# A product with wv by seven block products instead of eight, on one core

## The chip, the core and the metric

The kernel runs on one core of a Trainium2 chip. The core has TensorE (PE, matrix products), VectorE (DVE), ScalarE (ACT), GpSimd (POOL), SyncE (SP, which here only issues transfers) and 16 DMA engines. Each engine works through its own queue in order; semaphores make one wait for another. Products land in PSUM, which has eight banks of 128 x 512 numbers of 32 bits; everything else lies in SBUF. The metric is the device time in microseconds (us) of one execution.

## What is computed

Attention in blocks, a token and channel mixer, and a gated block follow each other. For 4 batches of 576 tokens with 512 channels:

```python
x = attention(q, k, v)                           # 8 heads of 64, mask by blocks of 64
xt = x.transpose(0, 2, 1)
h = np.maximum(xt @ w_tok1, 0.0) @ w_tok2
u = x + h.transpose(0, 2, 1)
u = u + np.maximum(u @ w_ch1, 0.0) @ w_ch2
x_prev = np.concatenate([zeros, u[:, :-1, :]], axis=1)
xk = mu_k * u + (1.0 - mu_k) * x_prev
xr = mu_r * u + (1.0 - mu_r) * x_prev
k = np.maximum(xk @ w_k, 0.0)                    # 512 to 1024
v = k * k @ w_v                                  # 1024 to 512
r = 1.0 / (1.0 + np.exp(-(xr @ w_r)))
return (r * v).astype(np.float32)
```

The change is in the line of v.

## The kernel before

**Tiling.** Channels lie on partitions, tokens along the row. The 2,304 tokens are eight tiles `t` of T = 288, two per batch; `u[b]` holds a batch's activations. Every dense product is done three times with numbers split into a high and a low part (high x high, high x low, low x high), by `dense`: three matmuls of 128 x 128 weights on 128 x 288 operands for each block of 128 channels.

**Weights.** They arrive from the host as 64-bit numbers, in pages of 128 rows and 512 columns. `page_ops` makes each page into a high and a low part: a load on SP (`l`), two conversions (`d0` on ACT or POOL, `d1` on ACT), the packing on DVE in two instructions (`d2`, lines 453 and 454), an addition on POOL (`d3`, line 458), the rounded copy (`hi`, line 182 on POOL, 178 on ACT) and the subtraction (`lo`, line 185, on DVE or POOL). Pages c1 and c2 are the channel mixer's, k, r and v the last block's. The last block's pages take the places of the channel mixer's as those come free.

**The last block.** For each tile: `xa` and `xm` (lines 757 and 761) mix neighbouring tokens, the result is split (`xsh`, `xsl`); K is eight blocks of 12 matmuls, `KR` the relu (line 786), `KS` the square (790), `KH` and `KL` its high and low part (797); R is four blocks of 12, `SG` the sigmoid; V is four blocks of 24 matmuls (`VO` for the first tile, by page: eight blocks of 12), and `Y` (843) multiplies V from PSUM with the sigmoid and sends it out. In TensorE's order a tile is K, R, V.

**Order.** Nothing is issued in the order of the code. `Plan` keeps a list of operations with engine, cost, dependences and priority, and lays them out one after another: of those that can start first on an engine, the one with the smallest priority number, to which the table `TILT` adds an offset by kind. Operations that may run on two engines go where the plan sees them end. Rings (PSUM banks, buffers) are resources of the plan. `record` then writes each engine's instructions in that order.

**PSUM.** The attention stage and the first channel-mixer tile use six single banks and one double bank (`ps1`); then `change2` releases them and a pool of eight banks follows.

Of the kernel before, what the change touches and what calls it, by code (L numbers as in the profile page):

```python
# [22 lines left out]
T = 288  # L23
# [22 lines left out]
TILT = {"ku": -1.2, "h1h": 0.5, "xl": -1.4, "n": -4.5, "h1l": -5.2, "xh": -1.6, "page-t2": 2.9, "xt": -0.6, "v": -2.0, "k2": 1.2, "q": 0.5, "rc": -3.6, "KH": 3.7, "KL": 0.2, "R": -1.5, "xa": 1.9, "page-v": 3.0, "O": 0.2, "V": -0.1, "Lh": -4.5, "xsh": -3.8, "U": -0.1, "C2": -4.8, "t": -14.0, "xm": 7.3, "K": 3.9, "z": 0.9, "page-c2": 4.3, "page-k": -1.7, "Ll": 13.8, "KS": -1.6, "page-c1": 2.6, "page-t1": -1.5, "xsl": 0.8, "load": 0.2, "L": 3.3, "e": 2.3, "page-r": -1.9, "pv": -0.2, "KR": -0.6, "m": -0.2}  # L46
# [6 lines left out]
class Plan:  # L53
# [8 lines left out]
    def __init__(self, tc):  # L62
        self.tc, self.last = tc, {}
        self.ops, self.users, self.rings, self.mode, self.slot = {}, {}, {}, {}, {}
# [4 lines left out]
    def add(self, name, engine, cost, deps, fn, pri, alloc=(), uses=(), lat=None, mode="f"):  # L69
# [3 lines left out]
        if kind in ("l", "d0", "d1", "d2", "d3", "hi", "lo"):  # L73
            kind = "page-" + name[1]
        elif kind == "v" and len(name) == 2:
            kind = "load"
# [35 lines left out]
    def run(self):  # L112
# [8 lines left out]
        self.taken = {t: [None] * n for t, n in self.rings.items()}  # L121
        self.order = []
# [47 lines left out]
def attn_mixer_rwkv_kernel(ctx: ExitStack, tc: tile.TileContext, z, v, wt1, wt2, wc1, wc2, wk, wv, wr, mu, out):  # L170
# [42 lines left out]
    u = [glob.tile([128, 4, S + 1], F32, name=f"u{b}") for b in range(B)]  # L213
# [23 lines left out]
    tl = {}  # L237


    def warm(k):  # L240
        t = ps1.tile([128, 512], F32, tag="s", bufs=6, name="warm")
# [23 lines left out]
    plan.ring("one", 6)  # L265
# [91 lines left out]
    def emit_pv(p, chunks):  # L357
        vt, vx = vs[p % 3], vd[p % 3]
        for i in chunks:
            part = int(i == 0)  # L360
            if ("pv", p, part) not in tl:
                tl["pv", p, part] = ps1.tile([128, 512], F32, tag="s", bufs=6, name="pv")
# [97 lines left out]
    def page_ops(name, src, n, room, pri, split_pri=None, gate=(), alloc=(), dense=False, late=False, slack=0.0):  # L460
# [28 lines left out]
        add(("hi",) + name, ("ACT", "POOL") if dense else "POOL", {"ACT": c_act(c), "POOL": c_pool1(c)}, [("d3",) + name], hi, sp, alloc=alloc, uses=[tk], lat=0.15 + 0.1 * slack)  # L489
# [408 lines left out]
```

## Time and profile before

| | |
|---|---|
| three runs, median (lowest to highest) | 820.31 us (819.71 to 820.81) |
| the profiled execution, its time | 821.57 us |
| its span, first to last instruction | 819.8 us |
| TensorE matmuls busy | 797.8 us (97%), 6,608 instructions |
| VectorE busy | 454.1 us (55%) |
| ScalarE busy | 355.5 us (43%) |
| GpSimd busy | 268.8 us (33%) |
| mean granted TensorE clock | 0.989 |

The stages in the trace: attention and the token mixer up to about 228 us, the channel mixer up to 548 us, the last block from there. Busy time counts the time in which an instruction runs; an instruction that has started and waits for access counts as busy too. An average over the span says little: the stages have different limits, so the windows by stretch and the waits of a stretch are read. A matmul's record of 0.3 us is its latency; the distance from one start to the next is the price.

### The profile page before, as it was taken

What the parts mean: (1) busy time and instruction counts of PE and PEld (TensorE: products, weight loads), DVE (VectorE), ACT (ScalarE), POOL (GpSimd) and SP (SyncE); (2) the same over time, 40 slices, a digit from 0 to 9 for tenths busy, and PEclk for the clock granted to TensorE, in tenths of its full rate; (3) what the DMA queues carried; (4) which work ended last, traced back from release to release, by engine and by line L of the source; (5) the groups of instructions that cost most, each with busy time, mean ns of one, the idle gap of its engine ahead of it and who ended that gap; (6) DMA issues with size and microseconds to landing.
All of it is one profiled execution on the core that took longest, in us unless ns stands there. A gap on an engine that the chain in (4) does not pass through costs nothing. (4 is left out here: it accounts for less than half of the span.)

```text
span 819.8 us, 16500 instructions
## 1 busy us (share of the span) xinstructions
PE 797.8 (97%) x6608; PEld 774.7 (95%) x6608; DVE 454.1 (55%) x1119; ACT 355.5 (43%) x913; POOL 268.8 (33%) x347
## 2 busy tenths in 40 slices
PE   7999999999998999999999999999699999999998
PEld 6898999999998989999999999998699999999998
DVE  5888877767777782212112124888963463553640
ACT  4786767666634451211111121444562362452530
POOL 4777764564666781101010102666400000000000
PEclk9999999999999999999999999999799999999999
DMA  6444323332124431000000000332000000000000
GB/s 175 136 128 138 99 79 106 98 89 90 37 71 152 156 123 58 1 1 2 1 1 1 1 2 27 104 105 102 26 6 30 22 10 30 15 15 30 9 22 30
DMA packets 34109, 47.60 MB, mean 58 GB/s; under 512 B 12912, under 2 KB 25200, under 8 KB 34032
## 3 DMA queue, kind: packets, MB, share of 16 engines
q1 hardware_dynamic: 34032, 46.54, 18.0%
q8 instruction: 52, 0.85, 0.4%
q14 instruction: 25, 0.20, 0.1%
HBM read 41.82 MB, written 4.72 MB: 57 GB/s over the span
## 5 line engine op out<-in xcount | busy, mean ns | idle before, releaser
L188 PE MATMUL b<-xhl,w 128*128 128x288 f32 x2304 | 312.4, 296 | 0.4 <-POOL xhl L686 0.4
L188 PEld LDWEIGHTS b<-xhl,w 128*128 128x128 f32 x2304 | 309.5, 188 | 0.6 <-POOL xhl L686 0.6
L188 PE MATMUL b<-hh,w 128*128 128x288 f32 x768 | 157.4, 298 | 4.5 <-DVE w L185 3.0
L188 PEld LDWEIGHTS b<-hh,w 128*128 128x128 f32 x768 | 125.1, 190 | 5.4 <-DVE w L185 3.7
L711 ACT ACTIVATE hh<-b 128x288 fp32r<-128x288 f32 x96 | 39.4, 410 | 191.6 <-PE b L188 191.1
L188 PE MATMUL b<-kh,w 128*128 128x288 f32 x512 | 106.0, 300 | 8.4 <-POOL w L182 3.7
L188 PE MATMUL b<-hl,w 128*128 128x288 f32 x384 | 113.8, 296 | 0.0
L339 POOL TENSOR_SCALAR P<-P,st 128x320 f32<-128x320 f32 (+4 forms) x160 | 85.6, 554 | 67.7 <-ACT P L330 38.6
L330 ACT ACTIVATE P<-P,st 128x576 f32<-128x576 f32 (+4 forms) x160 | 88.5, 556 | 20.3 <-DVE st L325 18.8
L188 PEld LDWEIGHTS b<-kh,w 128*128 128x128 f32 x512 | 83.9, 191 | 9.8 <-POOL w L182 4.3
L714 DVE SCALAR_TENSOR_TENSOR hl<-b,hh 128x288 fp32r<-128x288 f32 x96 | 43.3, 454 | 74.2 <-ACT hh L711 73.8
L458 POOL TENSOR_TENSOR td<-td,raw 128x512 int32<-128x512 int32 (+2 forms) x53 | 66.3, 1251 | 53.3 <-DVE td L454 12.1
L188 PE MATMUL b<-kl,w 128*128 128x288 f32 x256 | 76.3, 298 | 0.0
L188 PEld LDWEIGHTS b<-hl,w 128*128 128x128 f32 x384 | 73.0, 190 | 0.0
L786 ACT ACTIVATE kr<-b 128x288 f32<-128x288 f32 x64 | 26.2, 410 | 91.3 <-PE b L188 91.0
L746 DVE TENSOR_TENSOR u<-b,u 128x288 f32<-128x288 f32 x32 | 14.1, 455 | 92.2 <-PE b L188 92.1
L686 POOL TENSOR_TENSOR xhl<-u,xhl 128x1152 fp32r<-128x1152 f32 x8 | 19.6, 2454 | 136.8 <-ACT xhl L683 136.8
L188 PE MATMUL cs<-z 64*128 64x64 f32 (+6 forms) x352 | 61.6, 357 | 0.0
L843 DVE TENSOR_TENSOR o<-b,sg 128x288 f32<-128x288 f32 x32 | 14.4, 457 | 72.0 <-PE b L188 72.0
L348 PE MATMUL pt<-ident,P 128*128 128x128 f32 x320 | 47.9, 281 | 3.0 <-POOL P L339 3.0
L325 DVE CUSTOM_DVE_ANT_0 P<-cs,mask 128x448 f32<-128x448 f32 (+3 forms) x128 | 49.5, 415 | 2.1 <-PE cs L188 1.8
L454 DVE SCALAR_TENSOR_TENSOR td<-raw,td 128x512 uint32<-128x512 uint32 (+2 forms) x53 | 48.2, 910 | 1.8
(82 smaller groups left out, 1251.9 us busy)
## 6 DMA issues: line engine op xcount, KB each, us to landing
raw<-in_wc SPq DMA_DIRECT2D x24, 512.0 KB, 3.4
z<-in_z SPq DMA_DIRECT2D x16, 576.0 KB, 3.7
out<-o SPq DMA_DIRECT2D x32, 144.0 KB, 1.8
vs<-in_v SPq DMA_DIRECT2D x16, 256.0 KB, 3.2
raw<-in_wk SPq DMA_DIRECT2D x8, 512.0 KB, 3.2
raw<-in_wv SPq DMA_DIRECT2D x8, 512.0 KB, 3.2
vd<-in_v SPq DMA_DIRECT2D x32, 80.0 KB, 3.1
raw<-in_wr SPq DMA_DIRECT2D x4, 512.0 KB, 3.3
```

What stands on the lines that cost most here:

```text
L188: PE.matmul(o, lhsT=l, rhs=r, start=start, stop=stop)
L325: DVE.tensor_tensor_reduce(p_view(p, h, i), s_view(p, h, i), m, -0.125, 3.0e38, ALU.add, ALU.min, tl["st", p, h][:, 0, i:i + 1])
L330: ACT.activation(w, w, ACTF.Exp, bias=st[:, 0, i:i + 1], scale=-1.0, accum_out=st[:, 1, i:i + 1])
L339: POOL.tensor_scalar(w, w, tl["st", p, h][:, 2, i:i + 1], 1.0, ALU.mult, ALU.mult)
L348: PE.transpose(t[:, o + 128 * k:o + 128 * k + 128], tl["P", p, i][:, c:c + 128], ident)
L454: DVE.scalar_tensor_tensor(td, hw, 0x80000000, td, ALU.bitwise_and, ALU.bitwise_or)
L458: POOL.tensor_tensor(td.bitcast(I32), td.bitcast(I32), lw, ALU.add)
L686: POOL.tensor_tensor(tl["xhl"][i][:, 1], src(), f32(tl["xhl"][i][:, 0]), ALU.subtract)
L711: ACT.activation(tl["h", t, f][0], tl["lb", t, f][:, 0:T], ACTF.Relu)
L714: DVE.scalar_tensor_tensor(tl["h", t, f][1], tl["lb", t, f][:, 0:T], 0.0, f32(tl["h", t, f][0]), ALU.max, ALU.subtract)
L786: ACT.activation(tl["kr", t, f], tl["kb", t, f][:, 0:T], ACTF.Relu)
L843: DVE.tensor_tensor(o, src, tl["sg", t, m], ALU.mult)
```

## The change

The product of a batch's squared k (1,024 x 576) with wv is cut in quadrants: k by halves of the 1,024 channels and by the two token tiles (B11, B12, B21, B22), wv by halves of its rows and columns. Seven products of quadrants, `PROD`, replace eight. Their operands are B11, B21, B22, the differences T1 = B12 - B11, T2 = B22 - T1, T3 = B22 - B12, T4 = B21 - T2 (`TS`), and sums of wv's quadrants (`weight_sums`, made once, two pages at a time; `vc` and `vd` are the new pages). Each product is 4 x 2 blocks of three matmuls. The products are added up in `u` (`EV`: `s1`, `u2`, `u3`, `c11` and so on), and `Y` multiplies there, after R. In TensorE's order a batch is now K of two tiles, seven products, R of two tiles.

`u` of the first batch gives its place to `vd`: it is sent to the output (`spill`) and fetched back into the second batch's place (`fetch`), so the batches run as 1, 2, 3, 0. `bank` takes all PSUM tiles from one ring of eight; the change of pools is gone. wv's pages are decoded ahead of wr's. `TILT` has new numbers for nearly all kinds, among them these:

```diff
-TILT = {"ku": -1.2, "h1h": 0.5, "xl": -1.4, "n": -4.5, "h1l": -5.2, ...
+TILT = {"ku": -6.8, "h1h": 4.5, "n": -7.3, "h1l": -19.7, ...
...
+    def bank(key):
+
+        i = plan.slot["one", key]
+        if i < 6:
+            return ps1.tile([128, 512], F32, tag="s", bufs=6, name="b")
+        if "wide" not in tl:
+            tl["wide"] = ps1.tile([128, 1024], F32, tag="cd", name="cd")
+        return tl["wide"][:, 512 * i - 3072:512 * i - 2560]
...
-    plan.ring("one", 6)
+    plan.ring("one", 8)
+    plan.held += [("one", i, "wide") for i in (6, 7)]
...
+    def weight_sums(j, e):
+        en = DVE if e == "DVE" else POOL
+        a, b = (tl["td", ("v", j + 4 * k)].bitcast(F32) for k in range(2))
+        w = tl["vsum", j] = tl["raw", ("v", j + 4)].bitcast(F32)
+        en.tensor_tensor(w[:, 0:256], a[:, 256:512], b[:, 256:512], ALU.add)
+        en.tensor_tensor(w[:, 256:512], w[:, 0:256], a[:, 0:256], ALU.subtract)
+        en.tensor_tensor(w[:, 512:768], b[:, 0:256], w[:, 256:512], ALU.subtract)
+        en.tensor_tensor(a[:, 256:512], a[:, 0:256], a[:, 256:512], ALU.subtract)
...
-    when = {"c1": 9.0, "c2": 20.0, "k": 100.0, "r": 110.0, "v": 120.0}
+    when = {"c1": 9.0, "c2": 20.0, "k": 100.0, "r": 120.0, "v": 110.0}
...
+    add("spill", "SP", c_dma(4 * S * 512), [("U", t, m) for t in range(2) for m in range(4)], spill, 60.0, lat=4.0)
+    add("fetch", "SP", c_dma(4 * S * 512), ["spill"] + [("Y", t, m) for t in range(2) for m in range(4)], fetch, 140.0, lat=4.0)
...
+    PROD = (("va", 0, "B11"), ("vc", 256, "T2"), ("va", 256, "T3"), ("vb", 0, "B21"), ("vb", 256, "T4"), ("vc", 0, "T1"), ("vd", 0, "B22"))
...
+            add(("K", t, f), "PE", C12, [(s, "r", t, 0, m) for s in ("xsh", "xsl") for m in range(4)] + [("hi", "k", f), ("lo", "k", f)]
+                + ([("K", t, f - 1)] if f else [("K", t - 1, 7)] if c else [("L", NT - 1, 11)] if t == 0 else [("V", i - 1, 6, 3)])
+                + ([("O", NT - 1, 11)] if t == 0 and f >= 3 else []),
...
+        def TS(e, i=i, j=0, x="", a="", d=""):
+            en = DVE if e == "DVE" else POOL
+            o = tl["op", i, x, j] = tl["op", i, "B12", j] if x == "T3" else g32(name=x)
+            en.tensor_tensor(o, tl["op", i, a, j], tl["op", i, d, j], ALU.subtract)
+
+        def VH(e, i=i, j=0, x=""):
+            tl["vh", i, x, j], tl["vl", i, x, j] = g32(F32R, "vh"), g32(F32R, "vl")
+            copy("ACT", tl["vh", i, x, j], tl["op", i, x, j])
+
+        def VL(e, i=i, j=0, x=""):
+            sub(e, tl["vl", i, x, j], tl["op", i, x, j], f32(tl["vh", i, x, j]))
+
+        def VV(e, i=i, n=0, j=0):
+            x = ops[n]
+            if j == 0:
+                tl["vb", i, n] = [bank(("vb", i, n, m)) for m in range(2)]
+            for m in range(2):
+                dense(tl["vb", i, n][m], [vcol(n, j, m)], [(tl["vh", i, x, j], tl["vl", i, x, j])], j == 0, j == 3)
...
+            def plus(d, n, q):
+                DVE.tensor_tensor(d, tl["vb", i, n][m][:, 0:T], q, ALU.add)
```

**TensorE, from the end of the channel mixer into the last block.** `xhl` are the two split inputs, `kh` and `kl` the parts of the squared k. Before:

```order
L188 MATMUL b<-hh,w 128x288
L188 MATMUL b<-xhl_3170,w 128x288 x96
L188 MATMUL b<-xhl_3171,w 128x288 x48
L188 MATMUL b<-kh,w 128x288
L188 MATMUL b<-kl,w 128x288
```

and now, with `vh` and `vl` the parts of a product's operand, and `cd` the two banks of the former double bank:

```order
L192 MATMUL b<-xhl_3123,w 128x288 x60
L192 MATMUL cd<-xhl_3123,w 128x288 x12
L192 MATMUL b<-xhl_3124,w 128x288 x12
L192 MATMUL cd<-xhl_3124,w 128x288 x12
L192 MATMUL b<-xhl_3124,w 128x288 x60
L192 MATMUL cd<-xhl_3124,w 128x288 x12
L192 MATMUL b<-vh,w 128x288
L192 MATMUL b<-vl,w 128x288
```

Before, R of the first tile (48) stood between K (96) and the product with wv; now K of the second tile (96) does, and R has moved behind the products.

**VectorE, in the same place.** Lines 453 and 454 are a page's packing, 790 the squares, 797 a low part. Before:

```order
L790 TENSOR_TENSOR kr<-kr 128x288
L797 TENSOR_TENSOR kl<-kr,kh 128x288
L790 TENSOR_TENSOR kr<-kr 128x288
L185 TENSOR_TENSOR w<-td,w 128x512
L453 TENSOR_SCALAR td<-raw 128x512
L454 SCALAR_TENSOR_TENSOR td<-raw,td 128x512
```

Now, where 521 to 524 are `weight_sums`, 871 the squares, 910 `TS`, 468 and 469 the packing:

```order
L189 TENSOR_TENSOR vl<-kr,vh 128x288
L521 TENSOR_TENSOR raw<-td 128x256
L522 TENSOR_TENSOR raw<-raw,td 128x256
L523 TENSOR_TENSOR raw<-td,raw 128x256
L524 TENSOR_TENSOR td<-td 128x256
L871 TENSOR_TENSOR kr<-kr 128x288
L468 TENSOR_SCALAR td<-raw 128x512
L469 SCALAR_TENSOR_TENSOR td<-raw,td 128x512
L189 TENSOR_TENSOR w<-raw,w 128x512
L189 TENSOR_TENSOR vd<-raw,vd 128x256
L871 TENSOR_TENSOR kr<-kr 128x288 x3
L910 TENSOR_TENSOR T_6780<-kr 128x288
```

The sums of weight blocks, their low parts and the differences of operands have come in between squares and packing.

**GpSimd, at the start of the channel mixer.** `xhl <- u` is the low part of a whole token tile (the third here), 458 the addition and 182 the copy of a page. Before:

```order
L182 TENSOR_SCALAR w<-td 128x512
L445 TENSOR_SCALAR raw<-raw 128x512
L686 TENSOR_TENSOR xhl_3170<-u_59,xhl_3170 128x1152
L458 TENSOR_TENSOR td<-td,raw 128x512
L182 TENSOR_SCALAR w<-td 128x512
```

and now:

```order
L460 TENSOR_SCALAR raw<-raw 128x512
L473 TENSOR_TENSOR td<-td,raw 128x512
L186 TENSOR_SCALAR w<-td 128x512
L189 TENSOR_TENSOR w<-td,w 128x512
L473 TENSOR_TENSOR td<-td,raw 128x512
L186 TENSOR_SCALAR w<-td 128x512
L460 TENSOR_SCALAR raw<-raw 128x512
L730 TENSOR_TENSOR xhl_3123<-u_59,xhl_3123 128x1152
```

Five operations on the first two c2 pages now stand ahead of the token tile's low part, where they stood behind it.

## Rows read from the trace of the kernel before

**Rows 1.** Windows: stretch and length, busy us (instructions) by engine, TensorE clock, DMA.

```profile
256.00:268.00 12.00, 9.26 (x56) 8.79 (x55) 10.64 (x10) 4.41 (x10) 10.88 (x9) 0.86 0.36 114
514.50:589.20 74.70, 66.34 (x485) 64.94 (x483) 67.66 (x93) 36.79 (x79) 49.55 (x44) 0.96 0.26 85
600.00:800.00 200.00, 200.00 (x1506) 200.00 (x1505) 97.67 (x226) 88.09 (x226) 0.00 (x0) 1.00 0.06 19
```

**Rows 2.** The chain of waits in order of time, its end: start us, us, what.

```profile
589.21 227.33 PE b L188 x1690
...
816.63 0.46 DVE o L843
```

**Rows 3.** Timeline of TensorE: start us, us, operation, out<-in, shapes, count.

```profile
548.20 19.36 PE L188 MATMUL b<-xhl,w 128*128 128x288 f32 x144
567.39 0.29 PE L188 MATMUL b<-kh,w 128*128 128x288 f32 x1
```

**Rows 4.** Groups on TensorE, 480 to 600 us: busy us, mean ns, idle before them.

```profile
L188 PE MATMUL b<-kh,w 128*128 128x288 f32 x64 | 15.7, 331 | 8.4 <-POOL w L182 3.7 <-ACT kr L786 2.0 <-DVE w L185 1.7
```

**Rows 5.** Timeline of VectorE where GpSimd does not run a subtraction or addition.

```profile
557.52 0.44 DVE L790 TENSOR_TENSOR kr<-kr 128x288 f32<-128x288 f32 x1
557.89 0.41 DVE L453 TENSOR_SCALAR td<-raw 128x512 uint32<-128x512 uint32 x1
558.33 0.69 DVE L454 SCALAR_TENSOR_TENSOR td<-raw,td 128x512 uint32<-128x512 uint32 x1
558.94 0.45 DVE L790 TENSOR_TENSOR kr<-kr 128x288 f32<-128x288 f32 x1
...
588.48 0.68 DVE L185 TENSOR_TENSOR w<-td,w 128x512 fp32r<-128x512 f32 x1
589.08 0.45 DVE L185 TENSOR_TENSOR xhl<-xa,xhl 128x288 fp32r<-128x288 f32 x1
```

**Rows 6.** Timeline of VectorE, a packing step beside a GpSimd subtraction.

```profile
526.72 1.67 DVE L454 SCALAR_TENSOR_TENSOR td<-raw,td 128x512 uint32<-128x512 uint32 x1
```

**Rows 7.** Timeline of GpSimd; in brackets the idle time before and its cause.

```profile
255.24 2.46 POOL L686 TENSOR_TENSOR xhl<-u,xhl 128x1152 fp32r<-128x1152 f32 x1 [4.91 <-ACT xhl L683]
...
499.14 0.81 POOL L185 TENSOR_TENSOR xhl<-xa,xhl 128x288 fp32r<-128x288 f32 x1 [0.86 <-ACT xhl L178]
...
526.49 1.35 POOL L185 TENSOR_TENSOR w<-td,w 128x512 fp32r<-128x512 f32 x1
```

**Rows 8.** Groups on VectorE, 514.5 to 589.2 us, by shape.

```profile
L454 DVE SCALAR_TENSOR_TENSOR td<-raw,td 128x512 uint32<-128x512 uint32 x16 | 13.9, 871 | 0.6
L453 DVE TENSOR_SCALAR td<-raw 128x512 uint32<-128x512 uint32 x16 | 12.3, 767 | 0.8 <-POOL w L185 0.8
L185 DVE TENSOR_TENSOR w<-td,w 128x512 fp32r<-128x512 f32 x9 | 10.2, 1131 | 7.5 <-POOL w L182 5.7 <-ACT w L178 1.8
L761 DVE SCALAR_TENSOR_TENSOR xa<-u,mu_sb,xa 128x288 f32<-128x288 f32 x11 | 9.2, 879 | 0.0
L797 DVE TENSOR_TENSOR kl<-kr,kh 128x288 fp32r<-128x288 f32 x8 | 8.1, 1052 | 0.0
L185 DVE TENSOR_TENSOR xhl<-xa,xhl 128x288 fp32r<-128x288 f32 x10 | 7.3, 753 | 0.0
L790 DVE TENSOR_TENSOR kr<-kr 128x288 f32<-128x288 f32 x8 | 5.4, 691 | 0.0
L714 DVE SCALAR_TENSOR_TENSOR hl<-b,hh 128x288 fp32r<-128x288 f32 x11 | 4.7, 445 | 0.0
L746 DVE TENSOR_TENSOR u<-b,u 128x288 f32<-128x288 f32 x4 | 1.5, 444 | 0.0
```

**Rows 9.** Groups on GpSimd, 514.5 to 589.2 us, by shape.

```profile
L458 POOL TENSOR_TENSOR td<-td,raw 128x512 int32<-128x512 int32 x16 | 22.3, 1392 | 20.3 <-ACT xa L757 4.2 <-PE b L188 4.0 <-ACT kr L786 4.0
L185 POOL TENSOR_TENSOR w<-td,w 128x512 fp32r<-128x512 f32 x10 | 14.2, 1420 | 13.9 <-ACT w L178 13.2
L182 POOL TENSOR_SCALAR w<-td 128x512 fp32r<-128x512 f32 x16 | 11.7, 732 | 1.4
```

More of the change, by code (lines that the diff above doesn't have):

```diff
@@ L62, in __init__ @@
     def __init__(self, tc):
-        self.tc, self.last = tc, {}
+        self.tc, self.last, self.held = tc, {}, []
         self.ops, self.users, self.rings, self.mode, self.slot = {}, {}, {}, {}, {}
@@ L72, in add @@
         kind = name if isinstance(name, str) else name[0]
-        if kind in ("l", "d0", "d1", "d2", "d3", "hi", "lo"):
+        if name[0] in ("hi", "lo") and name[1] in ("vc", "vd"):
+            kind = "page-v"
+        elif kind in ("l", "d0", "d1", "d2", "d3", "hi", "lo"):
             kind = "page-" + name[1]
@@ L121, in run @@
         self.taken = {t: [None] * n for t, n in self.rings.items()}
+        for tag, i, key in self.held:
+            self.taken[tag][i] = key
         self.order = []
@@ L212, in attn_mixer_rwkv_kernel @@
     glob = tc.alloc_tile_pool(name="glob", bufs=1)
-    u = [glob.tile([128, 4, S + 1], F32, name=f"u{b}") for b in range(B)]
+    u = [glob.tile([128, 4, S + 1], F32, tag=f"u{b}", bufs=1, name=f"u{b}") for b in range(B)]
     ident = glob.tile([128, 128], F32, name="ident")
@@ L263, in attn_mixer_rwkv_kernel @@
     plan.ring("cd", 1)
-    plan.ring("one", 6)
+    plan.ring("one", 8)
+    plan.held += [("one", i, "wide") for i in (6, 7)]
+    plan.users["wide"] = [("m", NP - 1, h, 4) for h in range(2)]
     plan.ring("cs", 3)
@@ L361, in emit_pv @@
             if ("pv", p, part) not in tl:
-                tl["pv", p, part] = ps1.tile([128, 512], F32, tag="s", bufs=6, name="pv")
+                tl["pv", p, part] = bank(("pv", p, part))
             t, o = tl["pv", p, part], max(0, 128 * i - 128)
@@ L644, in change1 @@
         pools["w2a"] = xp
-    def change2(e):
-        ps1.release()
-        pools["ps"] = tc.alloc_tile_pool(name="ps2", bufs=1, space=PSUM, reuse_waits="tile")
     def change2s(e):
@@ L655, in attn_mixer_rwkv_kernel @@
     add("x2s", "NONE", 0.0, ["x1"] + last_tok, change2s, -99)
-    add("x2", "NONE", 0.0, ["x2s"] + [("Ll", 0, f) for f in range(12)], change2, -99)
-    plan.ring("b", 8)
     plan.ring("g", 28)
@@ L726, in O @@
                 if f == 0:
-                    tl["ob", t] = [bank(False) for _ in range(4)]
+                    tl["ob", t] = [bank(("ob", t, m)) for m in range(4)]
                 for m in range(4):
@@ L749, in attn_mixer_rwkv_kernel, with vpage, vslot @@
+    def vpage(n, j):
+        nm = PROD[n][0]
+        return [(s_, "v", j + 4 * (nm == "vb")) if nm in ("va", "vb") else (s_, nm, j) for s_ in ("hi", "lo")]
+    def vslot(n, j):
+        nm = PROD[n][0]
+        return ("W", "v", j + 4 * (nm == "vb")) if nm in ("va", "vb") else ("W", nm, j)
     for t in range(NT):
-        b, c = divmod(t, 2)
-        p0 = 130.0 + 8 * t
+        i, c = divmod(t, 2)
+        b = order[i]
+        ub = home[b]
+        p0 = 130.0 + 16 * i + 3 * c
         us, pr = slice(1 + T * c, 1 + T * c + T), slice(T * c, T * c + T)
-        ud = [("U", 2 * b + k, m) for k in range(c + 1) for m in range(4)]
+        ud = [("U", 2 * b + k, m) for k in range(c + 1) for m in range(4)] + ["fetch"] * (b == 0)
@@ L815, in SG, with Y @@
                 ACT.activation(tl["sg", t, m], tl["rb", t, m][:, 0:T], ACTF.Sigmoid)
+            def Y(e, t=t, m=m, b=b, c=c, ub=ub):
+                o = ub[:, m, 1 + T * c:1 + T * c + T]
+                DVE.tensor_tensor(o, o, tl["sg", t, m], ALU.mult)
+                SP.dma_start(out=out[128 * m:128 * m + 128, b, T * c:T * c + T], in_=o)
             key, sk = ("rb", t, m), ("sg", t, m)
[L818 to L819 removed]
+            add(("R", t, m), "PE", C12, [(s, "r", t, 1, m) for s in ("xsh", "xsl") for m in range(4)] + [(s, "r", k) for s in ("hi", "lo") for k in range(4)]
+                + [("V", i, 5, 3)] + ([("R", t, m - 1)] if m else [("R", t - 1, 3)] if c else []),
+                RR, 130.0 + 16 * i + 10 + c + 0.1 * m, alloc=[("one", key)], uses=[("x", "r", t, 1)] + [("W", "r", k) for k in range(4)], lat=0.3)
```

231 lines of the change are left out of this document (141 added, 90 removed).

## The prediction, made before the changed kernel ran

> **What bounds the kernel now.** The table of the profile says that TensorE is busy for 97% of the span, so I read first where it is not. The windows by stage come first [rows 1]: from 600 to 800 us TensorE has no idle time at all while VectorE is busy for 97.7 us of 200, so there the time is the number of matmuls. Two stretches are different: 256 to 268 us (9.26 us busy of 12, granted clock 0.86) and 514.5 to 589.2 us (66.3 of 74.7, clock 0.96). The chain of waits [rows 2] says the same: from 589.21 us to the end it is TensorE alone, and the last step is one VectorE multiplication at 816.63 us. Before 589.21 us the chain runs over VectorE. The second stretch is the hand-over from the channel mixer to the last block: the pages of wk, wr and wv are decoded there while TensorE already needs them.
>
> **The hand-over before, in numbers.** K and R of the first token tile start at 548.20 us, 144 matmuls in 19.19 us up to the next one, so 0.133 us each [rows 3]. From there to 816.57 us stand 1,920 matmuls (8 tiles of 96 + 48 + 96), 255.4 us at that pace, in 268.4 us: the hand-over costs 13.0 us. Of these 8.4 us are seen as waits ahead of the matmuls on kh [rows 4]. The last wait ends at 589.21 us, where the matmuls on the last wv page (228 blocks of 0.133 us after 548.20, so due at 578.5) start 10.7 us late; the other 2.3 us are the lower clock.
>
> What holds the pages up is VectorE together with GpSimd. VectorE operations alone take, start to start, 0.37 us (288 wide), 0.44 + 0.61 us (the two packing steps of a page) and 0.60 us (low part of a page, 512 wide) [rows 5]. The same second packing step takes 1.67 us at 526.72, where a GpSimd subtraction runs, and ends 0.55 us after that has ended [rows 6, 7]. From 514.5 to 589.2 us VectorE's own work is 16 x 1.05 (packing) + 9 x 0.60 (low parts) + 37 x 0.38 (288 wide from SBUF) + 15 x 0.37 (from PSUM) = 41.8 us [rows 5, 8]. It was busy for 67.7 us and idle for 7.0 us [rows 1], so 25.9 us of its busy time are waits behind GpSimd, which was busy for 49.6 us: 0.52 us of VectorE's time for each of GpSimd's.
>
> **The change part by part.** *Matmuls.* Each batch's product with wv has seven block products of 24 matmuls instead of eight: 4 x 24 = 96 fewer, 96 x 0.133 = -12.8 us. They all stand on the path once the hand-over is past, so this is worth its full price.
>
> *The hand-over after.* The order shows K of two tiles, then the seven products, then R of both tiles. Without any stall the last matmuls of the seventh product (354 matmuls after 548.20) are due at 595.3 us; before, the last wv page was due at 578.5. So the change gives 16.8 us more cover. Against this stands what VectorE has ahead of that operand in its order, counted from the same place as before (the second channel-mixer tile of the last batch): 16 page packings (16.8 us), 12 low parts (7.2), 2 of 256 columns (0.7), 16 additions on weight blocks (5.4, from 0.34 us each, 256 of 288 columns of [rows 5]), 70 operations of 288 columns (12 mixes, 6 low parts of x, 14 squares, 15 block differences, 23 low parts of operands: 26.6) and 23 from PSUM (8.5): 65.2 us instead of 41.8. GpSimd has, up to the same place, 16 additions and 11 subtractions of a page, 13 copies [rows 9], 14 operations of 288 columns at 0.81 [rows 7] and seven small ones (4.2 us together, an estimate from the same rows by width): 62.8 us instead of 49.6. At 0.52 us of waiting for each of these, VectorE needs 65.2 + 32.7 + 7.0 = 104.9 us from 514.5: 619.4 us, 24 us after the operand is due. I add 2 us because the fifth product's PSUM banks come free only after evictions that themselves wait for the last mix of R's input, and 3 us of low clock as before: 29 us instead of 13.0, so **+16 us**. From below: were VectorE not held more than before (25.9 us of waits), it would be done at 612.6, and if the new work also filled idle time, at 605.6, a hand-over of 13 to 20 us. From above: if every GpSimd operation shut VectorE out for its whole length, 56.7 us of VectorE work on SBUF and 62.8 us of GpSimd add up to 119.5 us, 634.0 us, a hand-over of 42 us. I take the middle because it is the one that reproduces the stretch before; the upper price would give 36.3 + 49.6 = 85.9 us for a stretch that took 74.7.
>
> The Trainium skill (SBUF — State Buffer, "SBUF: two separate sides") states that VectorE and GpSimd take a shared port pair as an exclusive lock, for a whole instruction. The trace shows the exclusion at single rows, but not for the whole length of each GpSimd operation. By the rule in full the sum would be the upper price above.
>
> *The channel mixer's start.* The trace has GpSimd idle for 4.91 us before 255.24 us, waiting for ScalarE's copy of x of the third token tile [rows 7]; the decoding of every c2 page queues behind that subtraction, and TensorE then has 56 matmuls in 12 us at clock 0.86, where 90 fit: 4.5 us lost [rows 1]. In the new order the first two c2 pages, but for one low part, are decoded ahead of that subtraction. GpSimd's idle time is then used, but TensorE also starts on c2 two blocks earlier. I take -4 us, between 0 and -4.5.
>
> *The later batches.* Per batch VectorE gets about 104 operations of 0.37 to 0.38 us, 39 us of 60.6 us of matmuls (456 x 0.133), so rate is no limit. One chain is short: the second product needs, 42 matmuls (5.6 us) after the last K block, a low part that has eleven VectorE operations (4.1 us) and three of GpSimd (2.4 us) ahead of it, after some 0.6 us for a copy on ScalarE and the step between engines (an estimate from the 0.44 us of an operation of that size): 7.1 us, 1.5 us late in each of three batches. I take +4 us, from 0 to 9.
>
> *The rest.* The end: R is now last, so a sigmoid stands between the last matmul and the last multiplication: +0.5 us, by the 0.44 us of an operation of that size [rows 5]. The copy of the first batch's u to the output and back is two transfers of 1.2 MB on SyncE; the copy out is issued ahead of the last wk page and waits for additions that ended long before, the copy back has three batches of time: 0. Were the copy out late, the last wk page would be fetched late too, and its matmuls are due 84 blocks, 11 us, after 548.20. The attention stage is recorded in another order, but TensorE is issuing without a gap for nearly all of it; I put it at 0, within 2 us either way. One ring of eight PSUM banks replaces a pool change, on which no row shows a wait: 0.
>
> Sum: -12.8 + 16 - 4 + 4 + 0.5 = **+3.7 us**. The profiled execution took 821.57 us (its span is 819.8), 1.3 us above the median of 820.31; I put the sum on the median: 824.0 us.
>
> **The rivals.** *The hand-over is no dearer than before.* VectorE's own work (65.2 us) and GpSimd's (62.8) each fit into the 80.8 us from 514.5 to 595.3; if the added work falls into each other's gaps, the hand-over stays at 13 us. For it: 7 us of idle time on VectorE and 25 us on GpSimd in that stretch [rows 1]. Against it: VectorE's 25.9 us of waits. Time: 820.3 - 12.8 - 4 + 4 + 0.5 = 808.
>
> *Full exclusion* (slower). Every GpSimd operation keeps VectorE off SBUF for its whole length; the operands of the seventh product are then ready at 634 us, 13 us dearer than my sum: 837 us. It decides against the change as soon as the hand-over costs more than 25 us. The Trainium skill's rule on the shared pair, named above, is this one.
>
> *Later batches and the start.* The hand-over is as I have it, but the start gains nothing and each later batch loses 3 us: +4 and +5, 833 us.
>
> That the change doesn't do what it says is settled by the order: 672 matmuls read vh or vl, where 768 read kh or kl.
>
> **How the numbers follow.** My forecast has 0.48 and by itself 816 to 832 us (the hand-over from 21 to 37 us); the first rival 0.25, full exclusion 0.15, the later batches 0.12. About 0.2% (1.6 us) is what a measurement of this kernel can tell from no change. Faster by more: the first rival and a small part of the forecast, 0.30. Within: 0.13 from the forecast. Slower: the rest, 0.57. The range goes from 810 to 838: it holds the forecast, full exclusion and the later batches, and leaves out most of the first rival.
>
> **What would show it.** After the change the first matmul of the second batch's K some 90 us after the first of the first batch's, where a hand-over without a stall has 60.6; TensorE should be idle for some 25 us of it, mostly ahead of the matmuls on vh of the second, third and last products, released by VectorE or GpSimd. TensorE from there to the end: 182 us of matmuls and under 8 us of gaps. Between 250 and 270 us the clock should stay at 1.0. If that distance is under 77 us, the sum of VectorE's waits was wrong; if it is right but the end is late, the later batches were.

## The result

| | before | after |
|---|---|---|
| median (lowest to highest) | 820.56 us (819.71 to 821.54) | 830.34 us (829.57 to 830.77) |
| profiled execution, time | 821.57 us | 829.57 us |
| its span | 819.8 us | 827.8 us |
| TensorE matmuls | 6,608 | 6,512 |
| VectorE busy | 454.1 us | 530.6 us |
| GpSimd busy | 268.8 us | 306.6 us |

The change makes the kernel slower: ratio 1.0118, 95% interval 1.0100 to 1.0135. The forecast was 824.0 us in a range of 810 to 838; the direction was right and the range held the time, but of 9.8 us between the medians the forecast had 3.7.

The windows of the changed kernel answer to [rows 1] (stretch and length, busy us and instructions by engine, TensorE's granted clock, DMA share, GB/s):

```profile
256.00:268.00 12.00, 11.47 (x88) 11.23 (x86) 10.66 (x13) 7.09 (x13) 9.71 (x9) 1.00 0.33 102
514.50:621.00 106.50, 86.47 (x586) 84.20 (x585) 100.12 (x152) 48.39 (x111) 67.03 (x61) 0.90 0.18 60
620.00:800.00 180.00, 176.46 (x1315) 175.00 (x1314) 136.01 (x306) 97.60 (x254) 24.00 (x29) 1.00 0.08 27
```

The channel mixer's start is better. VectorE (the third busy column) has next to no time left from 514.5 to 621 us: 100.1 us busy of 106.5, where it had 67.7 of 74.7. After that TensorE is no longer without a gap.

The timeline of TensorE gives the stages: each pair of lines is the end of one kind of work and the start of the next (start us, us, operation, out<-in, count). They answer to [rows 3].

```profile
551.47 0.29 PE L192 MATMUL cd<-hh,w 128*128 128x288 f32 x1
551.60 0.56 PE L192 MATMUL b<-xhl,w 128*128 128x288 f32 x3
...
582.22 0.69 PE L192 MATMUL cd<-xhl,w 128*128 128x288 f32 x4
582.75 0.29 PE L192 MATMUL b<-vh,w 128*128 128x288 f32 x1
...
623.06 0.29 PE L192 MATMUL cd<-vh,vd 128*128 128x288 f32 x1
623.19 1.10 PE L192 MATMUL b<-xhl,w 128*128 128x288 f32 x7
...
635.73 0.43 PE L192 MATMUL cd<-xhl,w 128*128 128x288 f32 x2
635.99 0.30 PE L192 MATMUL b<-xhl,w 128*128 128x288 f32 x1
```

K of the first batch starts at 551.60 us, 3.4 us later than before; its seven products run from 582.75 to 623.19, R to 635.99, where the second batch's K starts. That is 84.4 us for 456 matmuls, 60.65 at 0.133 us: 23.7 us are lost, 10.7 more than the 13.0 of before. The waits listed below come to 16.7 us in the last block; most of the other 7.0 us is matmuls at a lower clock (granted 0.90 from 551.6 to 636 us). In brackets stand the idle time and what ended it; the first line is a wait in the channel mixer, the line at 583.15 is no wait:

```profile
526.08 1.24 PE L192 MATMUL cd<-xhl,w 128*128 128x288 f32 x5 [3.35 <-DVE hl L758]
...
569.94 2.51 PE L192 MATMUL cd<-xhl,w 128*128 128x288 f32 x12 [3.78 <-ACT kr L867]
...
583.15 0.29 PE L192 MATMUL cd<-vh,w 128*128 128x288 f32 x1
...
593.84 0.61 PE L192 MATMUL cd<-vh,w 128*128 128x288 f32 x1 [8.10 <-ACT kr L867]
598.79 0.40 PE L192 MATMUL b<-vl,w 128*128 128x288 f32 x1 [0.56 <-POOL vl L189]
601.18 0.40 PE L192 MATMUL b<-vl,w 128*128 128x288 f32 x1 [1.33 <-DVE vl L189]
610.50 0.40 PE L192 MATMUL b<-vh,w 128*128 128x288 f32 x1 [0.45 <-ACT u L934]
616.42 0.40 PE L192 MATMUL b<-vh,w 128*128 128x288 f32 x1 [2.46 <-DVE u L931]
```

The first is new: before, there was no wait between 480 us and the last block. VectorE has the page packing of the new order ahead of the low parts `hl` of the channel mixer, the second of which ends the wait:

```profile
522.17 0.41 DVE L468 TENSOR_SCALAR td<-raw 128x512 uint32<-128x512 uint32 x1
522.62 1.66 DVE L469 SCALAR_TENSOR_TENSOR td<-raw,td 128x512 uint32<-128x512 uint32 x1
524.20 1.09 DVE L189 TENSOR_TENSOR w<-td,w 128x512 fp32r<-128x512 f32 x1
...
525.59 0.44 DVE L758 SCALAR_TENSOR_TENSOR hl<-cd,hh 128x288 fp32r<-128x288 f32 x1
```

It costs 3.35 us of waiting and 1.6 us of low clock behind it (36 matmuls from 526.08 to 532.49 us, 4.8 us at full speed): 4.95 us. The two longest waits bear the name of ScalarE's relu `kr`, and each ends 0.05 to 0.06 us after a relu that reads `cd`. At 593.84 that is not the relu of their own bank: the first product adds to its bank in `cd` from 583.15 us on, and is stopped ahead of its last three matmuls. In `bank` two of the eight PSUM banks are the halves of one tile, `cd`, so the matmuls into one half wait for the relu that reads the other. This is read from the rows and the code; no run of the changed kernel has the halves in tiles of their own. In ScalarE's queue the relu at 593.39 stands behind casts of T2 and of R's input, which wait for VectorE:

```profile
587.71 0.43 ACT L182 CAST vh<-T 128x288 fp32r<-128x288 f32 x1 [2.64 <-DVE T L910]
588.05 0.66 ACT L464 ACTIVATE raw<-raw 128x512 int32<-128x512 uint32 x1
589.42 0.43 ACT L182 CAST vh<-T 128x288 fp32r<-128x288 f32 x1 [0.71 <-DVE T L910]
590.22 0.43 ACT L182 CAST xhl<-td 128x288 fp32r<-128x288 f32 x1 [0.37 <-DVE td L842]
591.02 0.43 ACT L182 CAST xhl<-td 128x288 fp32r<-128x288 f32 x1 [0.37 <-DVE td L842]
591.98 0.43 ACT L182 CAST xhl<-td 128x288 fp32r<-128x288 f32 x1 [0.54 <-DVE td L842]
592.32 0.40 ACT L867 ACTIVATE kr<-b 128x288 f32<-128x288 f32 x1
592.95 0.54 ACT L838 ACTIVATE td<-u,om_sb 128x288 f32<-128x288 f32 x1 [0.23 <-DVE xhl L189]
593.39 0.39 ACT L867 ACTIVATE kr<-cd 128x288 f32<-128x288 f32 x1
```

So most of the 8.10 us is not ScalarE's work: it is idle for 4.9 us in between, each time for VectorE. They are VectorE's, one queue further on. The shared tile alone did not make the delay: the second product is held again at 601.18 us, by a low part that VectorE makes only then.

**Where the 8.0 us between the spans are.** Matmuls -12.8; the hand-over 10.7 in the last block and 4.95 ahead of it; the later batches 6.1 (the second to the fourth batch from 635.99 us to the last matmul, 188.1 us for 182.0); the sigmoid 0.5; the channel mixer's start -2.5; the attention stage 0.9. For the last two: from the channel mixer's first matmul (227.35 us before, 225.06 after, with 24 token-mixer matmuls, 3.2 us, more still to come) to K the losses are 7.3 us before and 9.8 after, of which the 4.95 are told already. The sum is 7.9.

### The profile page after: what moved, and what is told of

It is laid out like the page before. It is cut to its first block, busy times and chain, and to the rows that moved or that the text cites. A ratio compares the mean times of both kernels' runs of the same rounds, so it can differ in the third digit from the quotient of the medians.

```text
span 827.8 us, 16613 instructions
## 1 busy us (share of the span) xinstructions
PE 791.2 (96%) x6512; PEld 764.0 (92%) x6512; DVE 530.6 (64%) x1269; ACT 372.7 (45%) x973; POOL 306.6 (37%) x393
## 4 chain that ended last, share of the span: by engine, by line
PE 80%; DVE 14%; issue 3%; ACT 1%; POOL 1%; DVEq 0%; ACTq 0%; POOLq 0%
PE b L192 57%; PE cd L192 16%; PE b L363 5%; DVE td L468 3%; DVE td L469 2%; DVE w L189 1%; DVE kr L871 1%; DVE vl L189 1%; PE b L365 1%; PE b L572 1%; DVE T L910 1%; DVE P L340 1%; DVE kr L910 0%; DVE hl L758 0%; DVE raw L522 0%
## 5 line engine op out<-in xcount | busy, mean ns | idle before, releaser
L192 PE MATMUL b<-xhl,w 128*128 128x288 f32 x1728 | 240.9, 296 | 1.3 <-POOL xhl L730 1.3
L192 PEld LDWEIGHTS b<-xhl,w 128*128 128x128 f32 x1728 | 234.9, 189 | 1.5 <-POOL xhl L730 1.5
L354 POOL TENSOR_SCALAR P<-P,st 128x448 f32<-128x448 f32 (+4 forms) x160 | 84.1, 544 | 68.6 <-ACT P L345 25.6
L192 PE MATMUL cd<-xhl,w 128*128 128x288 f32 x576 | 86.4, 299 | 7.1 <-ACT kr L867 3.8
L192 PEld LDWEIGHTS cd<-xhl,w 128*128 128x128 f32 x576 | 80.8, 191 | 7.6 <-ACT kr L867 4.0
L192 PE MATMUL b<-vh,w 128*128 128x288 f32 x296 | 69.7, 306 | 2.9 <-DVE u L931 2.5
L192 PE MATMUL b<-z 64*128 64x64 f32 (+6 forms) x352 | 61.5, 357 | 0.0
L790 DVE TENSOR_TENSOR u<-b,u 128x288 f32<-128x288 f32 x25 | 11.1, 455 | 74.7 <-PE b L192 74.7
L189 POOL TENSOR_TENSOR xhl<-td,xhl 128x288 fp32r<-128x288 f32 x14 | 12.9, 923 | 117.9 <-ACT xhl L182 112.6
L192 PEld LDWEIGHTS b<-vh,w 128*128 128x128 f32 x296 | 52.4, 197 | 3.7 <-DVE u L931 2.7
L340 DVE CUSTOM_DVE_ANT_0 P<-b,mask 128x448 f32<-128x448 f32 (+3 forms) x128 | 49.5, 415 | 2.4 <-PE b L192 2.1
L363 PE MATMUL b<-ident,P 128*128 128x128 f32 x312 | 47.4, 282 | 2.7 <-POOL P L354 2.3
```

Of the source, the lines that this page charges most:

```text
L189: (DVE if e == "DVE" else POOL).tensor_tensor(o, a, b, ALU.subtract)
L192: PE.matmul(o, lhsT=l, rhs=r, start=start, stop=stop)
L340: DVE.tensor_tensor_reduce(p_view(p, h, i), s_view(p, h, i), m, -0.125, 3.0e38, ALU.add, ALU.min, tl["st", p, h][:, 0, i:i + 1])
L354: POOL.tensor_scalar(w, w, tl["st", p, h][:, 2, i:i + 1], 1.0, ALU.mult, ALU.mult)
L363: PE.transpose(t[:, o + 128 * k:o + 128 * k + 128], tl["P", p, i][:, c:c + 128], ident)
```

## The experiments

Two questions: is the hand-over bound by VectorE's load and its waits behind GpSimd (theory A), or by single waits in queues and rings (theory B)? And what holds the small terms? Theory C is full exclusion between VectorE and GpSimd.

**GpSimd's additions cut.** In the changed kernel and in the kernel before:

```diff
-    def dec3(raw, td):
+    def dec3(raw, td, n):
-        POOL.tensor_tensor(td.bitcast(I32), td.bitcast(I32), lw, ALU.add)
+        POOL.tensor_tensor(td[:, 0:n].bitcast(I32), td[:, 0:n].bitcast(I32), lw[:, 0:n], ALU.add)
...
+            lambda e: dec3(tl["raw", name], tl["td", name], 16 if name[0] in ("k", "r", "v") else c)
```

> The changed kernel, in the same order on every engine, but GpSimd's addition on a page of wk, wr or wv works on 16 of its 512 columns (the other columns keep the number without its low bits). Twenty additions of about 1.4 us become ones of about 0.2 us, an estimate from 0.81 us at 288 and 1.35 us at 512 columns: some 24 us of GpSimd's work is gone between 512 and 620 us. Theory A (the hand-over is bound by VectorE, whose operations wait 0.5 us for each us of GpSimd): about 12 us less waiting on VectorE, and the losses from 514 us to the second batch (28.7 us in the changed kernel) fall to 17: time about 818 us, 815 to 822. Theory B (the order and the buffers make the hand-over: relus queued on ScalarE, PSUM banks, 28 buffers): at most 3 us, 827 to 831. Theory C (every GpSimd operation shuts VectorE out for its whole length): over 20 us, below 811.

> The kernel before, in the same order, with the same cut of GpSimd's additions on the pages of wk, wr and wv to 16 columns. Sixteen of them lie between 514.5 and 589.2 us: 19 us of GpSimd's 49.6 are gone. Theory A: 10 us less waiting on VectorE, the hand-over of 13.0 us falls to 3 to 5: 811 to 814 us. Theory B: 818 to 821. Theory C: the hand-over is gone, 807 to 809.

Measured: the changed kernel 816.26 us (14.1 less), the kernel before 807.87 us (ratio 0.9845, interval 0.9831 to 0.986; 12.9 less than the runs of before beside it). Windows of the kernel before with this cut, and of the changed kernel with it:

```profile
514.50:580.00 65.50, 65.50 (x494) 65.50 (x493) 56.64 (x96) 36.14 (x79) 32.81 (x44) 1.00 0.31 100
...
514.50:589.20 74.70, 74.70 (x563) 74.70 (x562) 62.38 (x110) 42.10 (x94) 32.81 (x44) 1.00 0.29 93
```

```profile
514.50:606.00 91.50, 80.68 (x570) 78.96 (x569) 85.88 (x148) 48.07 (x111) 49.97 (x61) 0.94 0.20 70
```

In the first TensorE has no idle time at all where it lost 13 us [rows 1], although no operation of VectorE, TensorE or ScalarE is changed: without GpSimd's additions the hand-over of before is gone. Up to 580 us VectorE's own work is 42.6 us, by the durations of [rows 5], and its busy time 56.6, so it waits 14.0 us instead of 25.9 while GpSimd has 32.8 us instead of 49.6: 0.71 us for each us of addition taken away, more than the mean of 0.52. VectorE's idle time did not fall (7.0 us, now 8.9), so it is not that the pages came to VectorE sooner. In the changed kernel the time falls as theory A said; there VectorE's own work up to 606 us is 62.1 us, so it waits 23.8 us instead of 36.5, 0.75 us for each us of addition. Theory B is out for both; the time of the kernel before lies at theory C's price, but C in full asks for 85.9 us in a stretch that took 74.7, and for less than 811 us in the changed kernel.

**The weight sums cut** to 16 columns, in the changed kernel:

```diff
-        en.tensor_tensor(w[:, 0:256], a[:, 256:512], b[:, 256:512], ALU.add)
+        en.tensor_tensor(w[:, 0:16], a[:, 256:272], b[:, 256:272], ALU.add)
...
```

> The changed kernel, in the same order on every engine, but the sums of wv's quadrants work on 16 columns instead of 256. Theory A: 16 VectorE operations of 0.34 us become ones of under 0.1: 4.2 us of VectorE's own work are gone, the waits behind GpSimd stay what they are: 826 us, 824 to 828. If the waits go with the operations that have them (the four sums of one pair took 3.5 us together), 8 us: 822. Theory B (order and buffers): no change, 829 to 831.

The other columns of the sums are left out. Measured: 825.90 us, 4.4 less, theory A's number for VectorE's own work. K starts at 551.44 us and again at 631.99: the distance is 3.8 us shorter.

**The channel mixer's low parts first**, in the changed kernel. The order is laid out as it was, then recorded with the low parts (`Ll`) of the last tile moved:

```diff
+        late = {n for _, _, n in self.order if n[0] == "Ll" and n[1] == 7}
+        for _, e, n in self.order:
+            if n not in late:
+                self.record(ops[n][2], e)
+            if n[0] == "Lh" and n[1] == 7:
+                self.record(ops[("Ll",) + n[1:]][2], "DVE")
```

> The changed kernel with one thing moved: VectorE's low parts of the last channel-mixer tile stand right behind ScalarE's high parts, ahead of the page packing that the changed kernel has there. The wait of 3.35 us at 522.7 us, and the low clock behind it, should be gone, and K should start some 5 us earlier, at 546 to 547 us. Theory A (VectorE has no time left from 514 us to the second batch, so what it does earlier for one it does later for the other): from the first K to that of the second batch 88 to 90 us instead of 84.4, time 829 to 831 us. Theory B (the losses are single waits, each with its own cause): that distance stays at 84 to 85 us, time 825 to 826 us.

Measured: 829.25 us. The wait is gone, K starts 5.3 us earlier, and the second batch's K only 0.6:

```profile
546.26 0.43 PE L192 MATMUL b<-xhl,w 128*128 128x288 f32 x2
...
635.36 0.43 PE L192 MATMUL b<-xhl,w 128*128 128x288 f32 x2
```

89.1 us from K to K instead of 84.4: what VectorE does sooner for one it does later for the other. The 4.95 us in the channel mixer and the 23.7 in the last block are one cost.

**B21's product second**, in the changed kernel. The evictions are renumbered to match, and the plan lays the order out anew:

```diff
-    PROD = (("va", 0, "B11"), ("vc", 256, "T2"), ("va", 256, "T3"), ("vb", 0, "B21"), ...
+    PROD = (("va", 0, "B11"), ("vb", 0, "B21"), ("vc", 256, "T2"), ("va", 256, "T3"), ...
```

> The changed kernel with its products in another order: the one on B21, whose operand is there early, is second instead of fourth; the plan is laid out anew from there. In the changed kernel the products of the three later batches last 24.25, 23.95 and 24.67 us, where 168 matmuls at 0.1333 us take 22.4: 5.7 us lost, all ahead of the last operand of the second product. Theory A (that operand's chain is short of time by some 2 us, and 24 matmuls more ahead of it, 3.2 us, cover it): the three stretches come to 22.4 to 22.7 us, 5 us gained; in the hand-over, where the same operand is late by over 8 us, up to 3.2 more: time 822 to 825 us. Theory B (VectorE has too much to do in a batch of 60.6 us, so the wait moves to a later operand): the three stretches stay over 23.5 us, time 829 to 831.

Measured: 835.50 us, 5.2 more. The three later stretches of products grew from 24.25, 23.95 and 24.67 us to 26.2, 25.2 and 25.8. That is theory B of this run, and worse than it said. The added cover, with this new order, did not help; the waits are still for a low part, `vl`. Whether the move alone would help is not shown.

**The channel mixer's start**, in the kernel before, with GpSimd's low part of the third tile moved, and then with ScalarE's high part as well:

```diff
+        moved = ("xsl", "c", 2)
+        for _, e, n in self.order:
+            if n != moved:
+                self.record(ops[n][2], e)
+            if n == ("hi", "c2", 1):
+                self.record(ops[moved][2], "POOL")
```

> The kernel before with one move: GpSimd's low part of the third token tile stands behind the additions and rounded copies of the first two c2 pages instead of ahead of them; all other engines keep their order. Before, the stretch from the channel mixer's first matmul to its steady pace lost some 6 us, in the changed kernel some 2.5 us less of it. Theory A (the queue behind that low part is the cause): 2.5 to 4.5 us faster than before, 816 to 818 us. Theory B (the decoding of the c2 pages is late as a whole, the low part only stands there): within 1 us of before, 820 to 821.

> The kernel before, and the third token tile's high part on ScalarE and its low part on GpSimd both stand behind the first two c2 pages' conversions and additions. With the low part alone moved, GpSimd stood idle for 5.80 us all the same, waiting for ScalarE's conversion of the first c2 page, which is queued behind the copy of the token tile. Theory A (ScalarE's queue is the cause): that wait gets some 1.2 us shorter, the length of the copy, and with GpSimd's freed place the first c2 pages are 1 to 3 us sooner: 817.5 to 820 us. Theory B (the packing on VectorE, which stands behind that tile's last low parts there, holds the pages as well): within 1 us of before, 820 to 821.5.

Measured: 821.29 and 820.59 us, no difference from before (ratios 1.0004 and 0.9997, each within 0.13%). With the low part moved, GpSimd waits all the same (timeline of GpSimd, to be held against [rows 7]), and TensorE's waits come back elsewhere:

```profile
255.48 1.32 POOL L458 TENSOR_TENSOR td<-td,raw 128x512 int32<-128x512 int32 x1 [5.80 <-ACT raw L449]
...
260.14 0.53 PE L188 MATMUL b<-hh,w 128*128 128x288 f32 x2 [1.74 <-DVE w L185]
264.86 0.85 PE L188 MATMUL b<-hh,w 128*128 128x288 f32 x2 [2.68 <-POOL w L185]
```

With both moved, the two waits are 0.73 and 2.87 us, and GpSimd still waits:

```profile
254.96 1.33 POOL L458 TENSOR_TENSOR td<-td,raw 128x512 int32<-128x512 int32 x1 [4.73 <-ACT raw L449]
```

So neither run filled the idle time: behind the token tile's low part GpSimd waits for ScalarE's conversion of the first c2 page. The low part ahead of the pages was not what held them up.

**The first batch by eight products.** The kernel before up to its first batch, with its order and its PSUM banks in eight tiles, then seven products for three batches; the sums are made from the decoded pages during the first batch. `remake` adds a page's two parts; `weight_sums`, the new pages and the code of the changed kernel for tiles 2 to 7 follow it:

```diff
-    for t in range(NT):
+    for t in range(2):
...
+    def remake(e, j=0, k=0):
+        (DVE if e == "DVE" else POOL).tensor_tensor(tl["td", "s", j, k], f32(w[:, 0]), f32(w[:, 1]), ALU.add)
...
+    for t in range(2, NT):
```

> The kernel before up to the end of its first batch in the last block (eight products by page, K, R, V per tile, in its order), and the seven products for the other three batches. The sums of wv's quadrants are made from the decoded pages while TensorE works on the first batch; nothing is sent to the output and fetched back. 72 matmuls fewer than before: -9.6 us. Theory A (what the change lost is the hand-over, because VectorE's and GpSimd's added work stands there): the hand-over costs 13 us as before, the later batches lose 1.9 us each as in the changed kernel, the sigmoid at the end 0.5: 820.6 - 9.6 + 5.7 + 0.5 = 817 us, 815 to 819. Theory B (the seven products cost more than they save wherever they stand): 822 to 828.

> As the run with the first batch by eight products, and in the other three batches the product on B21 second. Theory A: the later batches' 5.7 us go as well: 812 us, 810 to 814. Theory B (VectorE's load in a batch): 816 to 818, no better than without the move.

Measured: 817.29 us (ratio 0.9953, 0.9938 to 0.9967), the time that theory A gave, and 821.77 us with B21 second. Of the first, the hand-over's window and one later batch's products:

```profile
514.50:589.20 74.70, 67.11 (x482) 65.71 (x481) 67.72 (x91) 37.39 (x82) 50.44 (x44) 0.95 0.26 86
```

```profile
712.28 0.29 PE L192 MATMUL b<-vh,w 128*128 128x288 f32 x1
...
736.08 0.29 PE L192 MATMUL b<-xhl,w 128*128 128x288 f32 x1
```

The window is that of [rows 1] nearly number for number, and the products take 23.8 us of 22.4. So the seven products do save their matmuls; what made the change slower is, in the main, where their preparation stands. B21 second costs again, 4.5 us: 2.9 in the three stretches of products, which take 24.7 us each, and the rest ahead of them, in an order laid out anew (K starts 1.1 us later).

**Other places for the differences**, in that kernel:

```diff
-            o = tl["op", i, x, j] = tl["op", i, "B12", j] if x == "T3" else g32(name=x)
+            if x == "T1":
+                tl["tt", i, j] = (wp if j < 2 else pools["w2a"]).tile([128, 512], I64, ...).bitcast(F32)
+            k = T * ("T1", "T2", "T4", "T3").index(x)
+            o = tl["op", i, x, j] = tl["op", i, "B12", j] if x == "T3" else tl["tt", i, j][:, k:k + T]
```

> As the run with the first batch by eight products, but the differences T1, T2 and T4 of the three later batches lie in the four places of the weights' raw pages, which are free by then, and no longer take twelve of the ring of 28 buffers. In the run without this the products of these batches lasted 23.8, 23.8 and 23.75 us where 168 matmuls take 22.4, and the relus of the last two K blocks waited for buffers that the first product releases. Theory A (the 28 buffers hold up the last operand of the second product, not VectorE's rate): the three stretches come to 22.4 to 22.7 us, 813 us, 812 to 814. Theory B (VectorE, busy for over 90% of the first part of that stretch, cannot be sooner): within 1 us of the run without, 816 to 818.

Measured: 815.24 us. The stretches are 23.34, 23.27 and 23.33 us, each 0.4 to 0.5 shorter, where theory A wanted 1.1 to 1.4. TensorE's waits from 640 to 820 us, in the run with eight products first and in this one:

```profile
PE b L192 <- DVE vl L189: 3.5, 3, 1.2
```

```profile
PE b L192 <- DVE vl L189: 2.2, 3, 0.8
```

The ring of 28 buffers, with the order that the plan laid out for this run, makes about a third of the later batches' loss in that kernel (1.4 us of 4.3); the rest is VectorE's queue, or the step from engine to engine, which these runs don't part.

**The pages' copies on ScalarE**, in the kernel before and in the version just told:

```diff
-            copy(e, w[0], tl["td", name].bitcast(F32))
+            copy("ACT" if name[0] in ("k", "r", "v") else e, w[0], tl["td", name].bitcast(F32))
```

> The kernel before with one group of instructions on another engine: the rounded copies of the pages of wk, wr and wv are made by ScalarE instead of GpSimd, all else in the same order. Sixteen copies of 0.73 us, 11.7 of GpSimd's 49.6 us from 514.5 to 589.2, go to ScalarE, which was busy for 36.8 of these 74.7 us and gets some 10 us more. Theory A (any us of GpSimd costs VectorE half a us): 6 us less waiting, the hand-over of 13.0 us falls to about 7: 814 to 816 us. Theory B (only GpSimd's operations with two operands hold VectorE up): within 1.5 us of before, 819 to 822.

> The run with the first batch by eight products and the differences in the raw pages' places (815.2 us), and the same copies on ScalarE. Theory A: its hand-over, 13 us as before, falls to about 7: 809 to 811 us. Theory B: 814 to 816.

Measured: 816.71 us (ratio 0.9955, 0.994 to 0.997) and 811.81 us (ratio 0.9894, 0.9877 to 0.991), the fastest kernel here that computes everything. Window of the kernel before with this change:

```profile
514.50:585.00 70.50, 67.03 (x483) 65.87 (x483) 63.62 (x91) 43.77 (x95) 38.71 (x28) 0.95 0.28 91
```

VectorE's own work up to there is 40.8 us, so it waits 22.8 us: 3.1 less for 10.8 us less on GpSimd, 0.29 per us. The result lies between the theories: a one-operand copy holds VectorE up too, but for less than half of what an addition does.

## Why the prediction was right and wrong

The direction was right, but the sum had 3.7 of 9.8 us. The steps that failed are small terms: the one ring of PSUM banks, put at nothing, cost about 2 us; the channel mixer's start, put at -4 us for a cause that the runs don't bear out, gave -2.5; the attention stage, put at nothing, cost 0.9.

**Right: the matmuls.** The first batch by eight products shows that they are saved: -9.6 us for 72 matmuls, +4.3 for the later batches and +0.5 for the sigmoid make -4.8, and -3.8 was measured against the runs of before beside it (821.06 us). That it met theory A's 817 us is in part luck: theory A had 5.7 us for the later batches.

**Right in size: the hand-over, +16 us.** It is 10.7 + 4.95 = 15.7 us. VectorE's part of the sum holds term by term. VectorE's groups up to the last product's operand, its largest ones (busy us, mean ns, idle before them; they answer to [rows 8]):

```profile
L469 DVE SCALAR_TENSOR_TENSOR td<-raw,td 128x512 uint32<-128x512 uint32 x15 | 15.1, 1004 | 0.5
L468 DVE TENSOR_SCALAR td<-raw 128x512 uint32<-128x512 uint32 x15 | 13.1, 875 | 1.2 <-POOL w L189 0.8
L871 DVE TENSOR_TENSOR kr<-kr 128x288 f32<-128x288 f32 x14 | 11.1, 822 | 0.0
L189 DVE TENSOR_TENSOR w<-td,w 128x512 fp32r<-128x512 f32 x8 | 8.2, 1020 | 0.7 <-ACT w L182 0.7
```

The counts of all its groups times the durations of [rows 5] give 63.6 us (65.2 in the forecast). It was busy for 100.1, so 36.5 us are waits, 0.55 for each of GpSimd's 67.0 us (0.52 forecast); with 6.4 us idle it was done at 621 us (619.4). That the rest adds up is in part luck: TensorE waits 20.0 us (16.7 + 3.35), where the sum had 26, and loses 8.6 us besides, most of it to the lower clock, where the sum had 3 "as before" (its own reading of before was 2.3). The banks' 2 us came as 0.45 and 2.46 us ahead of the fifth and the sixth product. The bounds of the term, 13 to 20 and 42 us, leave these 2 us out. The rival with the hand-over no dearer and full exclusion are both out. The mean coefficient hid two prices, 0.71 us for an addition and 0.29 for a copy; the mix of the two hardly changed, so the forecast did not suffer by it. The Trainium skill (SBUF — State Buffer, "SBUF: two separate sides") has an exclusive lock between GpSimd and those VectorE operations that read two inputs from SBUF or run in a two-port mode. Single rows agree (1.67 us for a packing step [rows 6]); over a stretch the price was about half of full exclusion, 0.52 and 0.55 us per us, and the measurement decides.

**Wrong in place.** I put the idle time ahead of the matmuls on `vh` of the second, third and last products. Part of it came in the channel mixer, and in K, and behind ScalarE's relus. I had counted VectorE's work ahead of one operand and not looked for who else waits in its queue. The moved low parts show that the total is the same wherever it is paid. For the same reason the distance from K to K is 84.4 us and not the 90 that were to show it. How much of the 8.10 us the ring of 28 makes in the first batch was not tried.

**Wrong: the channel mixer's start, -4 us.** It is -2.5 us, and the step failed at its reason. I took GpSimd's idle time ahead of the third tile's low part, and the queue behind it, for the cause; with that low part moved behind the pages the time is the same in two runs, and the idle time stays (4.91 us before, 5.80 and 4.73 us with the move), now for ScalarE's conversion of the page. In the changed kernel the first c2 page's load (the 13th of 24 in the order of the pages) is issued at 241.52 us instead of 244.66, and its packing starts at 249.54 instead of 253.22: 3.1 and 3.7 us earlier. That this makes the 2.5 us fits, but was only argued; the cause stays open.

**Too small: the later batches, +4 us.** They lose 6.1, of which 5.8 in the three stretches of products: 1.9, 1.6 and 2.3 us. The chain was right in its place and in its size: the waits for the second product's last low part are 1.18, 0.64 and 1.24 us, where the sum had 1.5 each (it did not have the ring of 28 buffers, which the ring run puts at 0.4 to 0.5 us per batch). The step that failed is "One ring of eight PSUM banks replaces a pool change": 0. The other 2 us are five short waits of matmuls into `cd`, four of which this view has:

```profile
PE b L192 <- DVE vl L189: 3.1, 3, 1.2
PE cd L192 <- DVE u L931: 0.5, 3, 0.2
PE cd L192 <- ACT kr L867: 0.2, 1, 0.2
```

Each stands in the middle of a product, on a bank that it has been adding to, and ends when an instruction that reads `cd` has ended (at 810.70 us in these rows of the timeline):

```profile
809.65 0.29 PE L192 MATMUL cd<-vh,vd 128*128 128x288 f32 x1
...
810.24 0.46 DVE L931 TENSOR_TENSOR u<-cd,u 128x288 f32<-128x288 f32 x1 [1.18 <-PE cd L192]
...
810.76 0.40 PE L192 MATMUL cd<-vh,vd 128*128 128x288 f32 x1 [0.16 <-DVE u L931]
```

The product's own bank can be read only after its last matmul, so what is read is the other half of the tile. From the start of one matmul to the next such a wait costs 0.4 to 0.5 us, the restart with it. The granted clock is 1.00 in all three stretches, so it has no part in this. With the first batch by eight products, where each bank is a tile, TensorE waits there for `vl` alone and loses 1.4 us per batch; but that kernel differs in its order too, and no run changes the tile alone. The reading that more cover would help got no support from B21's product second.

**Left at nothing: the attention stage**, 0.9 us within the 2 us given.

**The sum.** Forecast +3.7, spans +8.0: start 1.5, later batches 2.1, attention 0.9, all on the same side, hand-over -0.3. The remaining 1.8 us to the medians' 9.8 are the profiled executions: that of before lay 1.0 us above the median of 820.56, that of after 0.8 below its own. The start was taken near the kind end of its bounds (0 to -4.5); the middles of both bounded terms would have given 826.3. The rival of the later batches and the start (833 us) came nearer than the forecast, though each of its two steps went only about 40% as far as it said.

## What to carry to other kernels

A saving on TensorE is worth its price only in stretches that TensorE bounds: put the preparation that it needs where VectorE has time, here by computing the first batch the old way. In a stretch where VectorE has none left, count GpSimd's work as VectorE's too, by a coefficient taken from the stretch itself (0.5 here), and move what ScalarE can do. Don't take an idle engine in front of a late page for its cause: ask what the page would have waited for next. And give each PSUM bank a tile of its own, which was read from the trace here and not tried: a wait on a tile's name can be one for its other half.

## What the runs showed of the hardware

Taking additions off GpSimd beside a busy VectorE gave VectorE back 0.71 us per us (0.75 in the changed kernel), taking copies off 0.29. GpSimd's addition on 16 columns still takes 0.31 us, against 1.39 at 512 [rows 9]; group of the kernel before with the cut:

```profile
L458 POOL TENSOR_TENSOR td<-td,raw 128x16 int32<-128x16 int32 x16 | 4.9, 305 | 24.2 <-ACT kr L786 6.4 <-ACT xa L757 5.7 <-PE b L188 3.0
```

After the wait of 8.10 us TensorE's matmuls stand 0.24 us apart instead of 0.133 for some microseconds (594.24 to 597.36 us). The granted clock is 0.50 from 594 to 598 us, the level of 1.2 GHz of the two (1.2 and 2.4), and 0.59 in the window around it:

```profile
590.00:600.00 10.00, 5.45 (x22) 4.74 (x22) 9.86 (x15) 4.80 (x11) 6.58 (x7) 0.59 0.01 2
```
